# Unit 3's q and k turned by DMA, and a new hand-written order, in a fused gated-recurrence and MLP kernel

## The chip, the cores and the metric

The kernel runs on one core of a Trainium2 chip. The core has five engines that run side by side: TensorE (PE in the profile; it multiplies matrices and writes to PSUM), VectorE (DVE), ScalarE (ACT), GpSimd (POOL) and SyncE (SP, which here issues every transfer). Sixteen DMA engines move the data. PSUM has eight banks of 128 x 512 float32. The metric is the device time of one execution in microseconds; the median of several runs counts.

## The reference

Two stages: a recurrence with a decaying state for each of 4 x 8 heads over 768 steps, and an MLP with a leaky ReLU on its result for 3072 tokens.

```python
B, H, S, D = 4, 8, 768, 48
f = 1.0 / (1.0 + np.exp(-f_logit))
state = np.zeros((B, H, D, D), dtype=np.float32)
for t in range(S):
    state = f[:, :, t, :, None] * state + np.einsum('bhd,bhe->bhde', k[:, :, t], v[:, :, t])
    y[:, :, t] = np.einsum('bhd,bhde->bhe', q[:, :, t], state)
x = np.ascontiguousarray(y.transpose(0, 2, 1, 3)).reshape(B * S, H * D)
h = x @ w_in                        # (3072, 384) @ (384, 2048)
out = np.maximum(0.01 * h, h) @ w_out   # (3072, 2048) @ (2048, 384)
```

## The kernel before

**Units.** The sequence is cut into chunks of 128 steps. The work is 12 units of 256 tokens. Units 0 to 3 are "paired": unit j holds chunks 0 and 1 of batch j. Units 4 to 11 hold one chunk (2 to 5) of two batches. A call names its unit and mostly a half of it (0, 1, or 2 for both).

**One unit.** Loads `Lf Lk Lq Lv` bring f, k, q, v (line 186 for paired units, 190 for the others). ScalarE makes the log gate (`ge`, `gl`: lines 218 and 230). TensorE sums it over the chunk with a triangular matrix (`cs`, lines 239 to 250), ScalarE takes the exponentials (`dec`, lines 258 to 264), and VectorE or GpSimd multiplies them onto k and q (line 270, `k` and `q`; the last number of a call picks the engine: 0 VectorE, 1 GpSimd). The scaled k and q are needed with the head dimension on the partitions, so they are turned:

- by TensorE: `tk`, `tq` (line 304) transpose four blocks each into one PSUM bank, and `ck`, `cq` (lines 317 and 319) copy the bank to SBUF, on ScalarE or VectorE;
- by DMA: `xk`, `xq` (line 324), one transposing transfer from SBUF to SBUF for a whole unit, without TensorE, a bank or a copy.

Then follow the scores (`sc`, line 340 paired, 347 else), the causal mask (`mk`, VectorE, lines 357 and 361), the new state (`pt` on TensorE, `sf` on VectorE, line 466 or 468, `sb` on GpSimd, lines 473 and 476), and the mix of scores, values and earlier state into the unit's output (`mx`, and `ms` for the second chunk of a paired unit, line 378). `xt` (lines 438 and 440) copies that as xT, the input of the MLP.

**MLP of a unit.** Eight calls `up` (line 484, six matmuls each, weight piece g of `w_in`), each followed by a leaky ReLU on ScalarE (`pr`, line 489), then for each half four calls `dn` (line 496, four matmuls each), a copy (`ob`) and a store (`st`, line 511).

**Weights.** `WI` and `WO` load eight pieces each of `w_in` and `w_out` in float32 into the raw buffers of units 4 and 5; `ci` and `co` cast them to bf16. So a `WO` waits for the `ci` of the same place, and the loads of units 4 and 5 wait for the `co`. Raw buffers are six deep: the loads of unit j + 6 wait until unit j is scaled and cast.

**Order.** There is no automatic schedule. One string of words, `order`, is read from left to right, and every word issues its instructions at once on its engine; so the string fixes the order on each engine and of all transfers in SyncE's queue. Each engine runs its own list strictly in order and waits where data or a buffer is not ready. `F_n_512@b` puts n matmuls on zeros into bank b (line 96): work that only keeps TensorE running. The number behind `@` is the PSUM bank. `Z..` clears padding, `M..` makes constants.

Line 329 says where a turned unit lies, whichever way it was turned:

```python
def turn_dma(x):
    def go(j):
        nc.sync.dma_start_transpose(out=turned(j, x), in_=scaled(j, x).rearrange("t a h d -> t (a h d)"))
    return go
...
for word in order.split():
    word, _, on = word.partition("@")
    name, *numbers = word.split("_")
    parts[name](*[int(n) for n in numbers], *[int(n) for n in on.split(".") if n])
```

Of the kernel before, what the change touches and what calls it, by code (L numbers as in the profile page):

```python
# [15 lines left out]
def kernel(  # L16
# [527 lines left out]
    sc_2_0@5.7 mk_2_1_1 dn_0_1_0@0 mk_2_0_0 dn_1_1_0@6 ci_6_1 Lk_3_1 sf_2_0 dn_0_0_0@4 mk_2_0_1 sb_2_0
    dn_1_0_0@5 Lk_3_0 sf_2_1 up_0_6@3 mk_2_1_0 sb_2_1 up_1_6@7 co_2_0 pr_0_6 mx_2_2@1.2 pr_1_6 Lf_4_0 co_3_2
    ms_2 xt_2_0_0 dn_1_0_1 ge_3_1 xt_2_1_0 co_4_1 dn_1_1_1 WO_6 ge_3_0 up_2_2@3 gl_3_0 Lk_4_0 dn_0_1_1 gl_3_1
    co_5_1 pr_2_2 up_2_5@7 WO_7 cs_3_1@1 Lq_3_0 pr_2_5 up_2_6@2 Lq_4_0 up_2_0@3 pr_2_6 dn_0_0_1 pr_2_0 cs_3_0@7
    Lq_4_1 up_2_4@2 dec_3_0 up_2_1@3 k_3_0_0 ge_4_2 co_6_0 dn_0_1_2 gl_4_2 Lf_5_0 dn_1_1_2 pr_2_1 up_2_7@7
# [5 lines left out]
    cs_5_1@1 sb_3_0 mk_3_1_1 dn_2_1_1 Lk_5_1 dec_5_1 sf_3_1 dn_2_1_2 Lk_5_0 sb_3_1 dn_2_1_3 ge_6_2 dn_2_0_3  # L554
    gl_6_2 Lf_8_1 mx_3_2@3.6 ob_2_0_1 st_1_1 ms_3 xt_3_0_0 q_5_2_1 sc_4_2@5.7.4.1 Lq_7_0 xt_3_1_0 cs_6_1@2
    cs_6_0@3 mk_4_1_1 dec_6_1 up_3_3@6 mk_4_0_0 Lf_7_0 up_3_2@1 dec_6_0 mk_4_1_0 up_3_1@2 pr_3_2 mk_4_0_1
    up_3_6@5 Lv_4_0 pr_3_3 k_5_2_1 pr_3_1 up_3_0@3 Lv_4_1 pr_3_6 up_3_7@4 pr_3_0 up_3_5@1 pr_3_7 xq_5 dn_3_1_0@7
    pr_3_5 st_0_1 up_3_4@6 Lf_7_1 dn_3_1_1 pr_3_4 xk_5 dn_3_0_0@2 Lv_5_0 v_4_2_0 dn_3_0_1 dn_3_0_2 Lv_5_1
    dn_3_1_2 ob_2_1_1 dn_3_0_3 st_2_1 ge_7_2 dn_3_1_3 Lf_8_0 pt_4_0@5 gl_7_2 pt_4_1@3 Lv_8_0 sf_4_0 mx_4_2@4.1
    ob_3_1_1 sf_4_1 sb_4_0 sc_5_2@6.0.5.7 xt_4_0_1 cs_7_0@3 xt_4_1_1 mk_5_0_0 cs_7_1@4 sb_4_1 Lk_6_1 dec_7_0  # L560
    up_4_5@1 mk_5_0_1 Lk_6_0 up_4_0@6 dec_7_1 mk_5_1_1 v_5_2_1 mk_5_1_0 up_4_3@0 pr_4_0 up_4_2@3 st_2_0 pr_4_5
    Lq_6_1 pr_4_3 up_4_7@7 Lq_6_0 pr_4_2 up_4_6@4 ge_8_2 st_1_0 up_4_4@5 pr_4_6 up_4_1@6 Lk_7_0 gl_8_2 k_6_2_1
    Lf_10_0 pt_5_1@1 pt_5_0@0 pr_4_1 sf_5_1 mx_5_2@3.4 pr_4_4 sf_5_0 pr_4_7 sb_5_1 dn_4_0_0@6 xt_5_0_0 Lk_7_1
    dn_4_1_0@1 xt_5_1_1 sb_5_0 up_5_3@5 Lv_6_1 up_5_7@0 q_6_2_1 pr_5_3 cs_8_1@7 ob_3_0_1 Lq_7_1 up_5_6@3 pr_5_7
    up_5_0@4 dec_8_1 xk_6 dn_4_1_1 pr_5_6 xq_6 dn_4_1_2 pr_5_0 k_7_2_1 Lf_9_0 up_5_1@5 up_5_5@2 Lv_6_0 pr_5_1
    q_7_2_1 dn_4_1_3 pr_5_5 cs_8_0@0 xk_7 ob_4_1_0 up_5_4@7 dec_8_0 dn_4_0_1 pr_5_4 dn_5_0_0@3 dn_4_0_2 st_3_1
    dn_5_1_0@4 Lk_11_0 Lf_9_1 up_5_2@5 dn_4_0_3 xq_7 pr_5_2 v_6_2_0 sc_6_2@2.1.0.7 ob_4_0_1 dn_5_0_1 mk_6_0_1
    Lv_7_1 dn_5_1_1 mk_6_1_1 dn_5_1_2 mk_6_1_0 Lq_8_1 mk_6_0_0 dn_5_1_3 pt_6_0@5 Lq_8_0 dn_5_0_2 ob_5_1_1 sf_6_0
    ge_9_2 dn_5_0_3 sb_6_0 Lk_8_1 gl_9_2 pt_6_1@6 mx_6_2@1.7 sf_6_1 Lk_11_1 sc_7_2@0.2.4.5 sb_6_1 xt_6_0_1
    cs_9_1@6 xt_6_1_1 mk_7_1_1 cs_9_0@1 dec_9_1 up_6_5@7 mk_7_0_0 Lk_8_0 up_6_2@5 mk_7_0_1 dec_9_0 mk_7_1_0  # L570
    st_3_0 up_6_0@0 pr_6_5 q_8_2_1 Lf_10_1 up_6_3@6 pr_6_2 Lv_7_0 pr_6_0 up_6_4@2 pr_6_3 Lq_10_0 up_6_1@1 pr_6_4
    xq_8 up_6_7@4 pr_6_1 k_8_2_1 dn_6_1_0@7 ob_5_0_0 pr_6_7 dn_6_0_0@5 Lf_11_0 ge_10_2 dn_6_0_1 xk_8 gl_10_2
    v_7_2_1 dn_6_0_2 st_4_0 dn_6_1_1 Lv_8_1 pt_7_0@0 pt_7_1@6 cs_10_0@2 Lk_9_1 sf_7_0 dn_6_1_2 dec_10_0 sf_7_1
    sb_7_0 up_6_6@1 Lv_9_0 cs_10_1@3 pr_6_6 mx_7_2@4.0 sb_7_1 st_5_1 dec_10_1 dn_6_1_3 xt_7_0_1 dn_6_0_3
    xt_7_1_1 Lv_9_1 sc_8_2@6.2.1.3 ob_6_0_1 up_7_1@4 mk_8_0_0 st_4_1 up_7_7@0 mk_8_0_1 pr_7_1 Lq_9_0 mk_8_1_0
    up_7_2@5 pr_7_7 Lv_11_1 mk_8_1_1 up_7_3@6 pr_7_2 Lq_9_1 v_8_2_0 up_7_6@2 pr_7_3 Lf_11_1 up_7_4@4 pr_7_6
    v_9_2_0 pt_8_0@1 pt_8_1@0 pr_7_4 ob_6_1_0 up_7_0@3 Lk_9_0 sf_8_0 up_7_5@5 pr_7_0 sf_8_1 sb_8_0 Lk_10_1
# [51 lines left out]
```

## Time and profile before

| | |
|---|---|
| median of 3 runs | 179.4 us (179.13 to 181.27) |
| the profiled execution | 179.61 us |
| its span, first to last instruction | 177.8 us |
| TensorE matmul busy | 169.4 us, 95% of the span |
| transfers | 34.45 MB in 108186 packets, 152 issues by SyncE |
| transposing transfers | 16 (k and q of units 4 to 11) |

The profile shows one execution, from the first to the last instruction; the 1.8 us between time and span lie around it. "PE" is the matmul, "PEld" the weight load, which runs beside it. A group row gives line, engine, operation, output and input tiles, shape, count, busy time, mean duration in ns, and the idle time in front with what ended it. A window row gives start and end, the length, then the busy time of PE, PEld, DVE, ACT and POOL with instruction counts, the granted clock, the share of the DMA engines and GB/s. In the chain of waits each row is a start, a length, and the work that then set the end. In the timeline a row is a start, a length, the engine, the line and the instruction, and in brackets how long the engine stood before it and for what.

### The profile page before, as it was taken

What the parts mean: (1) busy time and instruction counts of PE and PEld (TensorE: products, weight loads), DVE (VectorE), ACT (ScalarE), POOL (GpSimd) and SP (SyncE); (2) the same over time, 40 slices, a digit from 0 to 9 for tenths busy, and PEclk for the clock granted to TensorE, in tenths of its full rate; (3) what the DMA queues carried; (4) which work ended last, traced back from release to release, by engine and by line L of the source; (5) the groups of instructions that cost most, each with busy time, mean ns of one, the idle gap of its engine ahead of it and who ended that gap; (6) DMA issues with size and microseconds to landing.
All of it is one profiled execution on the core that took longest, in us unless ns stands there. A gap on an engine that the chain in (4) does not pass through costs nothing.

```text
span 177.8 us, 5598 instructions
## 1 busy us (share of the span) xinstructions
PE 169.4 (95%) x2298; PEld 124.3 (70%) x2300; DVE 75.3 (42%) x168; ACT 113.1 (64%) x234; POOL 76.5 (43%) x138
## 2 busy tenths in 40 slices
...
GB/s 131 306 301 313 345 312 305 351 251 307 193 185 120 214 184 182 187 234 217 184 201 235 199 185 131 231 222 213 162 195 244 161 267 4 0 92 0 46 6 131
DMA packets 108186, 34.45 MB, mean 194 GB/s; under 512 B 100992, under 2 KB 107136, under 8 KB 108160
## 3 DMA queue, kind: packets, MB, share of 16 engines
...
q14 instruction: 8, 0.07, 0.1%
HBM read 25.17 MB, written 4.72 MB: 168 GB/s over the span
## 4 chain that ended last, share of the span: by engine, by line
PE 88%; SPq 5%; DMA 2%; issue 2%; ACT 1%; DVE 0%; ACTq 0%
PE ps L496 36%; PE ps L484 36%; PE ps L378 6%; SPq L186 5%; DMA f_raw<-in_f_logit_dram 2%; PE ps L347 2%; PE ps L247 2%; PE ps L304 1%; PE ps L456 1%; PE ps L340 1%; PE ps L451 1%; PE ps L96 1%; PE ps L250 1%; DVE kh L270 0%; ACT e L218 0%
## 5 line engine op out<-in xcount | busy, mean ns | idle before, releaser
L489 ACT ACTIVATE gT<-ps 128x512 bf16<-128x512 f32 x96 | 55.4, 615 | 27.4 <-PE ps L484 25.0
L496 PE MATMUL ps<-w_out,gT 128*128 128x384 bf16 x384 | 69.1, 327 | 0.0
L484 PE MATMUL ps<-xT,w_in 128*128 128x256 bf16 x576 | 68.8, 273 | 0.2 <-ACT xT L438 0.2
L484 PEld LDWEIGHTS <-w_in 128*128 128x128 bf16 x576 | 55.2, 98 | 9.1 <-DVE xT L440 0.2
L496 PEld LDWEIGHTS <-gT 128*128 128x128 bf16 x384 | 36.2, 98 | 21.7 <-ACT gT L489 0.3
L361 DVE TENSOR_TENSOR wm<-ps,ut 128x512 bf16<-128x512 f32 x32 | 20.0, 684 | 8.3 <-PE ps L347 8.3
L473 POOL TENSOR_TENSOR sf<-sf,end 128x192 f32<-128x192 f32 x16 | 8.1, 506 | 32.5 <-DVE sf L468 30.4
L270 POOL TENSOR_TENSOR kh<-k_raw,em 128x768 bf16<-128x768 f32 (+1 forms) x12 | 17.4, 1453 | 7.2 <-DMA k_raw<-in_k_dram 5.2
L468 DVE TENSOR_TENSOR sf<-sf,ps 64x192 f32<-64x192 f32 x32 | 11.2, 350 | 21.3 <-PE ps L456 16.3
L507 DVE COPY osb<-ps 128x384 f32<-128x384 f32 x9 | 4.9, 556 | 35.0 <-PE ps L496 26.6
L270 POOL TENSOR_TENSOR qh<-q_raw,at 128x768 bf16<-128x768 f32 (+1 forms) x10 | 15.0, 1496 | 9.2 <-DMA q_raw<-in_q_dram 8.8
L476 POOL CAST sb<-sf 64x192 bf16<-64x192 f32 x40 | 14.2, 355 | 8.2 <-DVE sf L466 5.7
L505 ACT COPY osb<-ps 128x384 f32<-128x384 f32 x15 | 7.3, 485 | 15.4 <-PE ps L496 8.4
L258 ACT ACTIVATE em<-ps 128x384 bf16<-128x384 f32 x24 | 12.1, 502 | 6.9 <-PE ps L250 3.4
L218 ACT ACTIVATE e<-f_raw 128x384 f32<-128x384 f32 (+1 forms) x16 | 11.0, 696 | 6.3 <-DMA f_raw<-in_f_logit_dram 6.1
L259 ACT ACTIVATE at<-ps 128x384 bf16<-128x384 f32 x24 | 12.1, 505 | 0.8 <-POOL qh L270 0.8
L230 ACT ACTIVATE lf<-e 128x384 bf16<-128x384 f32 (+1 forms) x16 | 10.6, 685 | 0.3
L357 DVE TENSOR_TENSOR wm<-ps,pair_mask 128x512 bf16<-128x512 f32 x16 | 10.4, 686 | 0.6 <-PE ps L340 0.3
L96 PE MATMUL ps<-zeros 128*128 128x512 bf16 x26 | 8.1, 458 | 1.3 <-DVE zeros L92 1.2
L438 ACT CAST xT<-ps 128x384 bf16<-128x384 f32 x13 | 6.2, 520 | 4.0 <-PE ps L378 3.9
L440 DVE CAST xT<-ps 128x384 bf16<-128x384 f32 x11 | 6.0, 572 | 6.0 <-PE ps L378 5.9
L378 PE MATMUL ps<-wm,v 64*32 64x128 bf16 (+1 forms) x256 | 7.5, 218 | 0.9 <-issue 0.9
...
## 6 DMA issues: line engine op xcount, KB each, us to landing
...
```

Of the source, the lines that this page charges most:

```text
L218: nc.scalar.activation(e[:, part], src[:, part], AF.Exp, scale=-1.0)
L230: nc.scalar.activation(dst, src, AF.Ln, bias=1.0)
L258: nc.scalar.activation(ems[j % 2][:, a], t[:, 0:H * D], AF.Exp, scale=1.0)
L259: nc.scalar.activation(ats[j % 2][:, a], t[:, 0:H * D], AF.Exp, scale=-1.0)
L270: eng.tensor_mul(heads(j, to[j % NR], a)[:, :, :, 0:D], raw_heads(j, x, a), decays(j, by, a))
L361: nc.vector.tensor_mul(w, src.rearrange("t (p n) -> t p n", p=P2), ut[:, None, :].to_broadcast([128, P2, 128]))
L378: nc.tensor.matmul(banks[st[j]["py", i]][32 * r:32 * r + 32, 128 * kk:128 * kk + 128], lhsT, rhs, start=(i, r) not in begun, stop=i in las ...
L468: nc.vector.tensor_add(sf[rows], sf[rows], new)
L476: nc.gpsimd.tensor_copy(out=sb[rows, :, y * D:y * D + D], in_=sf[rows])
L484: nc.tensor.matmul(pm[:, i, :], w_in_of(ff, kk), xTs[j % 3][:, kk].rearrange("t a s -> t (a s)"), start=(kk == 0), stop=(kk == NK - 1))
L489: nc.scalar.activation(gTs[j % 3][:, 2 * g:2 * g + 2, :], pm, AF.Prelu, alpha=0.01)
L496: nc.tensor.matmul(po, gTs[j % 3][:, ff, 128 * a:128 * a + 128], w_out_b[ff // 2][:, ff % 2, :], start=(ff == 0), stop=(ff == NF - 1))
```

## The change

Only the string `order` is replaced. The words of both strings name the same loads, gates, scores, mixes, ups, downs and stores, with these differences:

- unit 3 has no `tk_3`, `tq_3`, `ck_3`, `cq_3` (four turns and four copies) but `xq_3` and `xk_3`: 18 transposing transfers instead of 16;
- the fills are 7, 1, 2, 1, 1, 1, 1, 1 in eight places instead of 9, 4, 10, 2, 3 in five: 15 matmuls on zeros instead of 28;
- the order on every engine and in SyncE's queue, the engine of some casts, copies and products, and the banks are chosen anew. At the start the first 18 loads come first in SyncE's queue, as before, and then weight pieces 1, 5, 0, 7 (before: 5, 2, 0, 4, 1); in front of `cs_0_0` GpSimd now has six clears and the masks. Eight ups stand before the turns of unit 2 (`tk_2_1`). The mixes of units 9, 10 and 11 stand further forward.

In the diff every line is a piece of the string.

```diff
--- before.py
+++ after.py
@@ -526,71 +526,71 @@
     order = """
-    Zz F_9_512@7 Zb_1_0_1 Lf_0_1 Zb_2_0_0 Zl_1_0 Zb_2_1_0 Zk_2_1 Zv_1_0 Zq_2_0 Lf_0_0 Zl_2_0 Zb_3_0_1 Zb_0_0_0
-    Zk_0_0 Zq_1_0 Mt Lf_1_1 Zq_0_1 Lq_0_0 Zb_1_1_1 Zk_1_1 Lq_0_1 Zl_0_1 Mu Lf_1_0 ge_0_1 Lk_0_0 Zv_2_1 ge_0_0
-    Zb_3_1_1 Lk_0_1 Ms gl_0_0 Mp_0 Lv_0_1 gl_0_1 Mh Mi Lv_0_0 cs_0_0@0 Zb_0_1_1 ge_1_1 Mo Lf_2_1 Zv_0_1 cs_0_1@1
-    F_4_512@7 dec_0_0 Lv_1_1 Lq_1_1 dec_0_1 q_0_0_0 Lq_1_0 k_0_0_0 ge_1_0 Lk_1_0 gl_1_0 q_0_1_0 k_0_1_1 gl_1_1
-    Lf_2_0 tq_0_0@2 tq_0_1@3 cq_0_0_1 tk_0_0@4 Lv_1_0 cs_1_0@5 v_0_0_1 ck_0_0_1 cq_0_1_0 Lk_1_1 cs_1_1@6 v_0_1_0
-    dec_1_0 tk_0_1@7 WI_5 pt_0_2@0.1 ck_0_1_0 dec_1_1 WI_2 sc_0_0@2.3 sf_0_0 sc_0_1@4.5 F_10_512@7 WI_0 sb_0_0
-    mk_0_0_0 ge_2_1 WI_4 q_1_0_0 k_1_0_1 WI_1 sf_0_1 ge_2_0 Lq_2_0 mk_0_0_1 q_1_1_1 gl_2_0 WI_3 gl_2_1 mk_0_1_0
-    sb_0_1 tq_1_0@7 WI_7 cs_2_0@0 k_1_1_0 cq_1_0_1 tq_1_1@6 cs_2_1@2 dec_2_0 v_1_0_1 mk_0_1_1 tk_1_1@1 tk_1_0@3
-    dec_2_1 v_1_1_0 mx_0_2@4.7 cq_1_1_1 ci_5_0 Lk_2_0 pt_1_2@0.5 ck_1_0_1 xt_0_0_0 ms_0 F_2_512@3 ck_1_1_1
-    sf_1_0 ci_2_1 Lk_2_1 xt_0_1_1 sc_1_0@2.6 sc_1_1@3.4 mk_1_0_1 sb_1_0 up_0_5@1 mk_1_1_0 up_0_2@0 F_3_512@6
-    pr_0_5 mk_1_0_0 ci_0_1 Lv_2_1 pr_0_2 mk_1_1_1 up_0_0@7 sf_1_1 ci_4_1 Lq_2_1 mx_1_2@6.3 pr_0_0 sb_1_1 ci_1_2
-    Lv_2_0 ms_1 xt_1_0_0 up_0_4@1 q_2_0_1 xt_1_1_1 WO_0 up_0_1@2 ci_3_0 pr_0_4 WO_1 up_1_1@0 pr_0_1 up_1_0@4
...
-    dn_0_0_3 Lf_5_1 dec_4_1 dn_2_0_0@2 Lv_3_0 dn_1_0_3 Lv_3_1 ob_0_0_1 q_4_2_1 q_3_1_0 dn_1_1_3 Lq_5_0 Lf_6_1
-    dn_0_1_3 ob_1_1_0 k_4_2_1 tq_3_1@7 xq_4 ob_1_0_0 ob_0_1_1 tk_3_0@3 tq_3_0@1 ge_5_2 ck_3_0_0 up_2_3@4
-    cq_3_0_0 Lf_6_0 tk_3_1@6 gl_5_2 cq_3_1_0 dn_2_1_0@0 v_3_0_1 ck_3_1_0 v_3_1_0 pr_2_3 xk_4 sc_3_0@5.3
-    sc_3_1@1.7 mk_3_0_0 pt_3_2@6.4 mk_3_1_0 dn_2_0_1 mk_3_0_1 cs_5_0@5 st_0_0 dn_2_0_2 dec_5_0 sf_3_0 Lq_5_1
...
-    mk_10_0_1 up_9_0@6 mk_10_0_0 pr_9_6 mk_10_1_1 up_9_2@7 pr_9_0 ob_8_1_0 up_9_7@4 pr_9_2 st_8_1 up_9_3@2
-    ob_8_0_1 pr_9_7 st_8_0 up_9_4@1 pr_9_3 up_9_5@0 pr_9_4 up_9_1@6 pr_9_5 mx_10_2@5.7 pr_9_1 sc_11_2@3.4.2.1
-    xt_10_0_0 dn_9_0_0@0 mk_11_1_0 dn_9_1_0@6 mk_11_0_1 dn_9_1_1 xt_10_1_0 mk_11_0_0 dn_9_1_2 mk_11_1_1
-    up_10_1@5 up_10_4@2 pr_10_1 dn_9_0_1 pr_10_4 up_10_7@4 up_10_2@7 pr_10_7 up_10_6@3 pr_10_2 dn_9_1_3 pr_10_6
-    dn_9_0_2 ob_9_1_0 up_10_3@1 st_9_1 dn_9_0_3 pr_10_3 up_10_5@5 ob_9_0_1 up_10_0@2 st_9_0 pr_10_5 mx_11_2@4.7
...
+    Zz F_7_512@7 Lf_0_0 Lf_0_1 Lf_1_1 Lk_0_1 Lq_0_1 Lf_1_0 Lk_0_0 Lq_0_0 Lf_2_0 Lv_0_0 Lq_1_1 Lv_0_1 Lq_1_0
+    Lk_1_0 Lk_1_1 Lv_1_0 Lv_1_1 Lf_2_1 WI_1 WI_5 WI_0 WI_7 Lq_2_0 Lk_2_1 Lk_2_0 Lq_2_1 WI_2 Lv_2_1 Lv_2_0 WI_3
+    WI_4 Zq_0_0 ge_0_0 Zq_1_0 Zb_3_0_0 Zv_0_0 gl_0_0 ge_0_1 gl_0_1 ge_1_1 gl_1_1 Zq_2_1 Zv_2_1 Zb_1_0_1 Zk_2_0
+    Zl_1_0 Mt Zb_0_1_1 Zb_1_1_1 Zb_0_0_1 Zk_0_0 Zl_2_0 Ms Zl_0_0 Zb_3_1_0 Mu Mp_0 Mh cs_0_0@0 cs_0_1@1 F_1_512@7
+    dec_0_1 cs_1_1@2 k_0_1_0 q_0_1_0 Zb_2_1_1 Zb_2_0_0 dec_0_0 dec_1_1 Mi tk_0_1@3 ck_0_1_0 tq_0_1@4 F_2_512@0
+    cq_0_1_0 sc_0_1@5.6 F_1_512@4 mk_0_1_1 mk_0_1_0 q_0_0_1 tq_0_0@7 cq_0_0_0 v_0_0_0 ge_1_0 gl_1_0 cs_1_0@1
+    F_1_512@6 ge_2_0 gl_2_0 cs_2_0@0 v_0_1_0 dec_1_0 k_1_0_0 k_0_0_1 tk_0_0@3 ck_0_0_1 pt_0_2@4.2 F_1_512@1
+    sf_0_0 sc_0_0@6.5 F_1_512@3 mk_0_0_1 dec_2_0 mk_0_0_0 Zk_1_1 tk_1_0@7 ck_1_0_1 Zv_1_1 q_1_1_1 tq_1_1@1
+    cq_1_1_0 q_1_0_1 tq_1_0@3 cq_1_0_1 k_1_1_1 tk_1_1@0 F_1_512@5 sc_1_0@4.7 mk_1_0_1 mk_1_0_0 v_1_0_1
+    mx_0_2@5.3 ck_1_1_1 sc_1_1@6.0 mk_1_1_1 mk_1_1_0 ge_2_1 sb_0_0 ms_0 sf_0_1 v_1_1_1 pt_1_2@1.7 sf_1_0 gl_2_1
+    cs_2_1@4 xt_0_0_1 xt_0_1_1 ci_0_0 WO_0 ci_1_1 up_0_1@5 WO_1 mx_1_2@0.3 ci_5_1 pr_0_1 up_0_5@6 pr_0_5 sb_1_0
+    ms_1 xt_1_1_1 sf_1_1 up_0_0@2 pr_0_0 Lv_3_0 dec_2_1 ci_7_0 up_0_7@1 pr_0_7 xt_1_0_0 up_1_7@5 up_1_5@7
+    up_1_1@6 up_1_0@3 pr_1_5 pr_1_1 k_2_1_1 tk_2_1@0 ck_2_1_1 WI_6 k_2_0_0 tk_2_0@2 ck_2_0_1 pr_1_0 q_2_1_0
+    tq_2_1@4 pr_1_7 q_2_0_0 tq_2_0@1 ci_2_0 up_0_2@7 up_1_2@6 pr_1_2 Mo cq_2_0_0 sc_2_0@0.2 cq_2_1_0 sc_2_1@1.4
+    mk_2_0_0 WO_5 Lf_3_1 WO_2 sb_1_1 Lv_3_1 Lf_3_0 mk_2_1_0 v_2_1_1 v_2_0_1 pt_2_2@3.5 mk_2_1_1 Lq_3_1 ci_3_1
+    up_0_3@6 pr_0_3 up_1_3@0 WO_3 WO_7 ci_4_1 up_0_4@1 up_1_4@4 pr_0_4 WO_4 sb_0_1 Lk_3_0 sf_2_0 co_0_2 Lf_4_1
+    Lf_4_0 mk_2_0_1 mx_2_2@6.3 Lk_3_1 Lq_3_0 pr_1_4 pr_0_2 sb_2_0 ms_2 xt_2_1_1 sf_2_1 co_1_0 dn_1_1_0@2
+    dn_0_1_0@1 dn_1_0_0@5 dn_0_0_0@4 pr_1_3 xt_2_0_0 up_2_7@6 up_2_3@7 up_2_5@3 up_2_4@0 pr_2_7 up_2_2@6 pr_2_5
+    up_2_1@3 pr_2_3 up_2_0@7 co_5_0 v_3_0_0 sb_2_1 ge_3_1 pr_2_4 v_3_1_0 ci_6_1 up_2_6@0 WO_6 pr_2_1 up_1_6@3
+    gl_3_1 pr_2_2 cs_3_1@6 pr_2_6 up_0_6@0 co_2_1 Lq_4_1 Lq_4_0 co_3_0 dn_0_0_1 dn_0_1_1 dn_1_0_1 dn_1_1_1
+    dec_3_1 k_3_1_0 q_3_1_1 ge_3_0 gl_3_0 cs_3_0@6 dec_3_0 q_3_0_0 xq_3 k_3_0_0 xk_3 co_4_1 dn_1_1_2 Lf_5_0
+    dn_0_1_2 dn_1_0_2 dn_0_0_2 Lf_5_1 pr_0_6 pr_2_0 dn_2_0_0@6 dn_2_0_1 dn_2_0_2 pr_1_6 co_6_1 ge_4_2 gl_4_2
+    cs_4_1@0 dec_4_1 co_7_0 dn_0_1_3 dn_0_0_3 dn_1_0_3 ob_0_1_0 ob_0_0_1 ob_1_0_1 Lk_4_0 Lv_5_0 cs_4_0@7 dec_4_0
+    q_4_2_1 st_0_0 st_1_0 dn_1_1_3 ob_1_1_0 Lv_4_0 Lk_4_1 xq_4 pt_3_2@3.0 sf_3_0 sb_3_0 sc_3_1@1.4 mk_3_1_1
+    st_0_1 Lv_4_1 sc_3_0@5.7 mk_3_0_1 mk_3_0_0 mk_3_1_0 sf_3_1 dn_2_1_0@2 dn_2_1_1 dn_2_1_2 dn_2_1_3 mx_3_2@3.4
...
+    up_8_1@1 up_8_5@5 pr_8_1 up_8_4@4 pr_8_4 pr_8_5 mk_9_0_0 mx_9_2@7.0 xt_9_0_1 xt_9_1_1 up_8_0@1 pr_8_0
+    dn_7_0_3 ob_7_0_0 st_7_0 v_10_2_1 cs_10_0@2 dec_10_0 k_10_2_1 xk_10 q_10_2_1 xq_10 up_8_7@4 pr_8_7 up_8_3@5
+    pr_8_3 up_9_3@7 pr_9_3 up_9_6@0 pr_9_6 up_8_2@1 pr_8_2 pt_8_0@3 sf_8_0 sb_8_0 up_8_6@2 pr_8_6 cs_11_1@4
+    dec_11_1 q_11_2_1 xq_11 pt_9_1@5 sf_9_1 pt_8_1@7 k_11_2_1 xk_11 sf_8_1 sb_8_1 v_11_2_0 pt_9_0@0 sf_9_0
+    sb_9_0 dn_7_1_3 ob_7_1_0 st_7_1 up_9_0@1 pr_9_0 dn_8_1_0@3 up_9_2@2 pr_9_2 up_9_1@5 pr_9_1 up_9_4@4 pr_9_4
+    up_9_7@7 pr_9_7 dn_8_0_0@1 dn_8_0_1 sb_9_1 sc_10_2@0.2.6.5 mk_10_0_0 mk_10_1_1 mk_10_1_0 mk_10_0_1 up_9_5@4
+    pr_9_5 dn_8_1_1 dn_9_0_0@7 dn_9_0_1 sc_11_2@0.5.4.6 mk_11_1_0 mk_11_0_1 mk_11_1_1 mk_11_0_0 dn_8_0_2
+    dn_8_0_3 ob_8_0_0 st_8_0 dn_9_1_0@2 mx_10_2@4.5 xt_10_0_0 xt_10_1_1 mx_11_2@6.0 xt_11_1_0 xt_11_0_1 dn_8_1_2
+    up_10_1@1 pr_10_1 up_10_4@5 pr_10_4 dn_9_0_2 up_11_0@4 pr_11_0 dn_9_1_1 up_11_4@6 pr_11_4 up_11_3@0 pr_11_3
...
     """
```

75 lines of the change are left out of this document (31 added, 44 removed).

## Prediction

> **What bounds the kernel now.** I read the page's busy times and its chain of waits first, then the windows, the chain in order of time, and the timeline of the first 25 us.
>
> ```profile
> PE 169.4 (95%) x2298; PEld 124.3 (70%) x2300; DVE 75.3 (42%) x168; ACT 113.1 (64%) x234; POOL 76.5 (43%) x138
> ...
> PE 88%; SPq 5%; DMA 2%; issue 2%; ACT 1%; DVE 0%; ACTq 0%
> ...
> L489 ACT ACTIVATE gT<-ps 128x512 bf16<-128x512 f32 x96 | 55.4, 615 | 27.4 <-PE ps L484 25.0
> ```
>
> ```profile
> 0.00:24.67 24.67, 19.74 (x373) 12.56 (x375) 16.52 (x50) 17.86 (x42) 17.36 (x51) 1.00 0.98 284
> 24.67:174.64 149.97, 149.70 (x1933) 111.77 (x1926) 58.76 (x119) 94.79 (x192) 59.10 (x87) 1.00 0.82 180
> ```
>
> TensorE has 88% of the chain. In the second window it is busy 149.70 of 149.97 us: from 24.67 us to the last matmul there is nothing to win except by giving it less to do. What can move is the first 25 us, where the busy time includes fills on zeros. Two things count: the time T at which the unbroken stretch begins, and how many `up` calls lie before it.
>
> ```profile
> 0.00:24.67 24.67, 2.31 (x19) 1.69 (x19) 1.00 0.98 284
> ```
>
> ```profile
> 24.73 6.66 PE ps L484 x60
> ...
> 31.39 0.89 PE ps L304 x16
> ...
> 69.48 4.55 PE ps L496 x28
> ...
> 100.37 0.90 PE ps L378 x56
> 101.27 0.55 PE ps L347 x16
> ...
> 157.91 0.90 PE ps L378 x56
> ...
> 174.64 0.48 ACT osb L505
> ```
>
> The row that stands alone is line 484 by itself, up to 24.67 us. An `up` is 6 matmuls, so 3 ups come before the stretch (the 19th matmul opens it). Besides, TensorE has by then done all gate sums of units 0 to 2 and all turns, scores, states and mixes of units 0 and 1. The chain gives its prices: an `up` 6.66/10 = 0.67, a `dn` 4.55/7 = 0.65, a mix 0.90, a score 0.55, sixteen turns 0.89.
>
> **The change, step by step.** The order strings hold the same 96 ups, 96 downs, 12 mixes and 16 scores; the differences are these.
>
> *Turns of unit 3.* Its four TensorE turns (16 matmuls) go: -0.89 us from a full engine, all gained. Their four copies were VectorE's, 42% busy, and gain nothing. In their place SyncE issues two transposes.
>
> ```profile
> qT<-qh SPq DMA_TRANSPOSE x8, 3.7
> kT<-kh SPq DMA_TRANSPOSE x8, 4.0
> ```
>
> ```profile
> 141.07 1.92 SPq L324 DMA_TRANSPOSE qT<-qh  x1
> ```
>
> The last transpose of all took 1.92 us to issue; I take that for each at most, and 4 us to landing. They wait for the scaled q and k of unit 3, and SyncE's loads of units 5 and 4 queue behind them. Adding prices along the new order of TensorE from T = 25.0, the second half of unit 3's gate sum ends at 44.5; after two exponentials (each at most a relu's 0.6) and two VectorE products (each about 0.58, the cast of the same size below) k's transpose is ready at 46.9, issues behind q's at about 48 and lands at 52. The score wants it at 52.7. So the two cost nothing, with 0.7 us in hand; anything later stops TensorE by its excess. Upper end: all of one landing, 4 us.
>
> *Fills.* Before there are 28, now 15. All stand ahead of T, where TensorE waits for others: 0 us, as long as the clock stays up (rivals).
>
> *The first 25 us.* SyncE sends 18 loads of units 0 to 2 first, then four weight pieces, as before but in another order (pieces 1, 5, 0, 7). So I take the landing times of the same places in the queue.
>
> ```profile
> 8.83 0.92 POOL L270 TENSOR_TENSOR kh<-k_raw,em 128x384 bf16<-128x384 f32 x1 [1.39 <-DMA k_raw<-in_k_dram]
> ...
> 13.53 0.92 POOL L270 TENSOR_TENSOR kh<-k_raw,em 128x384 bf16<-128x384 f32 x1 [1.09 <-DMA k_raw<-in_k_dram]
> ...
> 18.01 1.05 POOL L166 CAST w_in<-q_raw 128x768 bf16<-128x768 f32 x1 [0.15 <-DMA q_raw<-in_moe_w_in_dram]
> 19.17 0.81 POOL L476 CAST sb<-sf 64x192 bf16<-64x192 f32 x2
> ```
>
> ```profile
> 17.82 0.55 DVE L166 CAST w_in<-k_raw 128x768 bf16<-128x768 f32 x1
> 18.29 0.58 DVE L440 CAST xT<-ps 128x384 bf16<-128x384 f32 x1
> 18.78 0.72 DVE L466 TENSOR_TENSOR sf<-ps,end 64x192 f32<-64x192 f32 x2
> 19.75 2.48 DVE L357 TENSOR_TENSOR wm<-ps,pair_mask 128x512 bf16<-128x512 f32 x4 [0.25 <-PE ps L340]
> ```
>
> ```profile
> 20.00:25.00 5.00, 4.06 (x100) 2.93 (x99) 3.33 (x7) 2.72 (x5) 3.04 (x6) 1.00 1.11 341
> ```
>
> Three waits on a transfer date the 8th, 15th and 20th load: 8.8, 13.5 and 18.0 us; so the 14th, half of unit 1's k, is there at 13.5 - 0.7 = 12.8. From it VectorE runs without a gap: product k 0.6 (as the 0.58 cast) to 13.4; state 0.72 to 14.1; two masks of 2.48/4 to 15.4; a turn's copy at most 0.58 to 15.9; four masks to 18.4; two state adds 1.44 to 19.9; weight piece 0, 0.55, to 20.4; one state 0.72 to 21.1; piece 7 (landed at 18.0 plus twice 393 KB at 341 GB/s, 20.3) to 21.7; unit 1's xT to 22.3. GpSimd casts unit 1's state for 0.81 after 19.9, so its last mix ends near 21.0. TensorE then does up 0 and up 7 of unit 0 by 22.3 and four ups of unit 1 by 25.0. This T is the choice on which the sum rests. Lower end: two weight pieces fewer in the way of xT and a 14th load at 12.5, 24.2; upper end: each of some ten hand-offs 0.15 us late, 26.5.
>
> At T the new order has done the same set plus 8 ups where the old had 3: 5 x 0.67 = 3.3 us less to do.
>
> *From T on.* Transfers: weight pieces 2, 3 and 4 land later than their ups would like, at about 24.4, 26.8 and 28 (one place in the queue costs 0.6 or 1.15 us at 341 GB/s), but each is cast under 1 us later and wanted at 25.9, 28.2 and 29.5. ScalarE: near 40 us unit 3's gate sums want a bank behind six relus (0.615 each) and two gate halves, and near 49 us unit 4's gate sum stands behind two whole gate passes; I put 0.7 us on these two places, between 0 (ScalarE idles 36% of the span) and 2 (three such waits of one relu each). Later loads: the new order mixes units 9, 10 and 11 earlier, the last at 142.5 us, where the old did it at 157.9. That needs the transposes of unit 11 at about 139, where the old order issued the last at 141.07. See the second rival.
>
> *Sum, against the profiled execution* (span 177.8, time 179.61): matmuls end at 25.0 + 149.97 - 3.3 - 0.89 - 0.27 (the old idle of that stretch) + 0.7 = 171.2. The end is the same copy, store and landing: 177.8 - 174.64 = 3.2, span 174.4. With the 1.8 us around the span, 176.2; the median of the runs is 0.2 below the profiled one: **176.0 us**, 1.9% less.
>
> **Rivals.**
>
> *1. The clock is not up in time.*
>
> ```profile
> 1.19 3.81 PE L96 MATMUL ps<-zeros 128*128 128x512 bf16 x9 [1.19 <-DVE zeros L92]
> ...
> 12.05 2.11 PE L96 MATMUL ps<-zeros 128*128 128x512 bf16 x9 [0.16 <-issue]
> ```
>
> Nine fills take 0.42 us each at the start and 0.23 each at 12 us: TensorE begins at half rate, and 3.8 us of fills brought it up. Now seven fills last 7 x 0.42 = 3.0 us, followed by a hole until GpSimd has made the masks, which it now does after six clears (about 5 us). If the rate stays half for the sparse work up to 18 us, the first links of the chain above are late by some of it, 0.3 to 1 us; if it is still half when the ups begin, another 3.8 us of work is done at half rate, 1.9. Middle: +1.5, so 177.5. For it: fewer fills, one at a time. Against it: the gate sums, turns and scores before 12 us are the same work as before, and the old order too had holes there. [...]
>
> *2. The transfers cannot be brought forward (the slower side).*
>
> ```profile
> SPq L324 <- POOL qh L270: 5.1, 3, 3.6
> SPq L324 <- POOL sf L473: 4.2, 2, 3.0
> SPq L324 <- POOL kh L270: 2.9, 3, 1.3
> ```
>
> SyncE's queue is strict in order. In the old run its transposes stood 12.2 us waiting for GpSimd in these three groups alone, with everything behind them. In the new order the queue after unit 3 sums to about 130 us for the last transpose if nothing waits, and by the gate sum of unit 11 (about 130.3, plus two exponentials of 0.6 and two GpSimd products of at most twice the 0.92 of half a unit) to about 135.2, landing at 139.2. The score of unit 11 is wanted near 139.8. If the queue collects the old 12.2 us of waits instead, that transpose issues at 142 and lands at 146: 6 us of TensorE standing, 182. Above 3.4 us of such standing the gain is gone; above 7 us it is slower by 2%. Against it: the wanted order leaves 2 to 5 us between landing and score at most units, by the same sums.
>
> *3. The lead is lost on the way:* one or two operands or banks that the order packs tightly (unit 3's transposes, 0.7 us in hand; unit 11's, 0.6) come 2 to 3 us late: 178.5 to 179.4, no change. That the turns and fills bring nothing by themselves is part of this.
>
> **How the numbers follow.** About 2%, 3.6 us, is what a measurement of this kernel can tell from no change; it lies at 175.8 and 183.0. My case has 0.66 (own range 174.2 to 177.5; the line at 175.8 cuts it nearly in the middle, 0.34 below and 0.32 above), the clock 0.13, the lost lead 0.12, late transfers 0.09, of which 0.07 beyond 183. Faster 0.34 + 0.02 from a mild form of the clock's case = 0.36; slower 0.07; the rest, 0.57, within. The range leaves out late transfers beyond 179.6 and what would need T below 24.2 and no new idle: 174.0 to 179.6.
>
> **What would show it.** Right: line 484 has some 48 matmuls before 25 us and a full stretch from there; turns of line 304 fall from 64 to 48; transposes from 16 to 18; idle from T to the end under 1.5 us. Wrong: T beyond 26; fills or turns at 0.42 us after 5 us (clock); a wait of line 340 or 347 for a transposed kT or qT of over 1 us; SyncE's transposes waiting longer than 12 us in sum.

## The result, and the profile after

| | before | after |
|---|---|---|
| median (4 runs each) | 179.26 us (179.03 to 181.27) | 185.28 us (184.32 to 186.29) |
| ratio | | 1.031, 95% interval 1.022 to 1.040 |
| the profiled execution, its span | 179.61 us, 177.8 us | 186.29 us, 184.5 us |

The change makes the kernel 3.1% slower. Where some runs of a kernel took over 1.5% longer than its fastest, the ratios and their intervals leave them out, while the medians are of all runs. The page of the changed kernel, beginning with the busy times; the second and third line are the busy tenths of TensorE and of the DMA engines in 40 slices of the span, the fourth is the transfer queue (packets, MB, share of 16 engines), the last the chain of waits:

```profile
PE 168.9 (92%) x2269; PEld 123.3 (67%) x2271; DVE 79.8 (43%) x172; ACT 109.4 (59%) x228; POOL 77.5 (42%) x136
...
PE   6768999999999989999999699989999779999991
...
DMA  5999999999197999999989999999978561011022
...
q1 hardware_dynamic: 110272, 34.61, 80.5%
...
PE 48%; SPq 15%; DMA 13%; POOL 10%; DVE 5%; issue 4%; ACT 3%; POOLq 0%; ACTq 0%
```

TensorE's part of the chain has fallen from 88% to 48%. SyncE's queue, transfers and GpSimd have taken it. The windows of the changed kernel, cut where the turns of unit 2 begin and at the last matmul; then line 484 alone in the first of them:

```profile
0.00:27.67 27.67, 22.27 (x390) 15.39 (x393) 21.51 (x56) 19.47 (x44) 17.69 (x47) 0.94 0.98 275
```

```profile
27.67:180.70 153.03, 146.60 (x1882) 107.94 (x1879) 58.29 (x117) 89.45 (x184) 59.78 (x90) 1.00 0.80 177
```

```profile
0.00:27.67 27.67, 5.76 (x48) 4.32 (x48) 0.94 0.98 275
```

The matmuls end at 180.70 instead of the 171.2 forecast. The 9.5 us divide into three: the stretch begins 2.67 late (27.67 for 25.0); TensorE stands 153.03 - 146.60 = 6.43 us in it, 5.7 more than forecast (it stood 0.27 before); its work there is 146.60 instead of 149.97 - 0.27 - 3.3 - 0.89 = 145.5, 1.1 more, for which no row gives a cause. Where it stands, and where SyncE does, from the waits of the changed kernel (sum, times, longest):

```profile
PE ps L347 <- DMA kT<-kh: 3.0, 2, 1.6
...
PE ps L347 <- DMA qT<-qh: 1.3, 2, 1.0
```

```profile
SPq L324 <- DVE qh L270: 6.1, 1, 6.1
```

SyncE's queue at two places, from the changed kernel's timeline:

```profile
41.97 1.00 SPq L190 DMA_DIRECT2D q_raw<-in_q_dram  x2
49.25 1.34 SPq L324 DMA_TRANSPOSE qT<-qh  x1
50.68 1.28 SPq L324 DMA_TRANSPOSE kT<-kh  x1
...
137.85 1.44 SPq L190 DMA_DIRECT2D v_raw<-in_v_dram  x1
139.39 0.65 SPq L511 DMA_DIRECT2D out_dram<-osb  x1
141.30 1.24 SPq L324 DMA_TRANSPOSE kT<-kh  x1
142.90 4.44 SPq L324 DMA_TRANSPOSE qT<-qh  x2
147.71 1.23 SPq L324 DMA_TRANSPOSE kT<-kh  x1
```

From 42.97 to 49.25 SyncE issues nothing: the first word in its way is unit 3's q transpose, whose product is not ready. Unit 11's k is transposed from 147.71 (its landing follows at 150.76), where the last transpose of the kernel before began at 141.07 and landed at 145.49. Now the windows of the kernel before, up to its last transpose's landing, where the last three numbers are granted clock, DMA share and GB/s:

```profile
5.00:145.49 140.49, 136.56 (x1969) 102.42 (x1970) 68.05 (x147) 96.84 (x206) 72.26 (x120) 1.00 1.01 228
```

```profile
42.97:49.25 6.28, 6.28 (x57) 4.86 (x55) 1.47 (x3) 5.18 (x13) 0.83 (x1) 1.00 0.99 209
49.25:145.49 96.24, 96.05 (x1285) 71.74 (x1284) 41.37 (x89) 63.77 (x134) 47.65 (x68) 1.00 0.99 196
```

and windows of the changed kernel:

```profile
42.90:49.30 6.40, 6.40 (x56) 4.53 (x54) 1.33 (x3) 4.19 (x12) 2.45 (x3) 1.00 0.54 137
```

```profile
42.97:49.25 6.28, 6.28 (x55) 4.41 (x54) 1.28 (x3) 4.07 (x12) 2.45 (x3) 1.00 0.55 138
49.25:150.76 101.51, 95.13 (x1258) 69.58 (x1256) 40.59 (x82) 64.21 (x134) 47.42 (x65) 1.00 0.98 196
```

```profile
5.00:150.76 145.76, 135.72 (x1934) 100.92 (x1936) 70.81 (x146) 95.42 (x204) 72.60 (x116) 0.99 0.98 223
```

In the kernel before, the 16 DMA engines are full on the mean of the 140 us up to the last transpose's landing (share 1.01; a value over 1 says that the measure is rough). TensorE was not the only bound: over this stretch the transfers were a second one. In the changed kernel the share falls to 0.54 while SyncE stands, 6.40 x 0.46 = 2.9 us of all engines lost.

These windows account for the late landing. Behind 49.25 us both kernels move 196 GB/s up to their last transpose's landing, and the changed kernel needs 101.51 us for it instead of 96.24. The 5.27 us more are 1.03 MB at that rate: 0.45 MB were not moved while SyncE stood (138 GB/s instead of 209 for 6.28 us), and 0.52 MB are the two added transposes (34.61 MB instead of 34.09).

### The profile page after: what moved, and what is told of

It reads as the page before. It is cut to its first block, busy times and chain, and to the rows that moved or that the text cites. A ratio compares the mean times of both kernels' runs of the same rounds, so it can differ in the third digit from the quotient of the medians.

```text
span 184.5 us, 5521 instructions
## 1 busy us (share of the span) xinstructions
PE 168.9 (92%) x2269; PEld 123.3 (67%) x2271; DVE 79.8 (43%) x172; ACT 109.4 (59%) x228; POOL 77.5 (42%) x136
## 3 DMA queue, kind: packets, MB, share of 16 engines
q1 hardware_dynamic: 110272, 34.61, 80.5%
## 4 chain that ended last, share of the span: by engine, by line
PE 48%; SPq 15%; DMA 13%; POOL 10%; DVE 5%; issue 4%; ACT 3%; POOLq 0%; ACTq 0%
PE ps L496 23%; PE ps L484 17%; SPq L190 8%; DMA k_raw<-in_k_dram 6%; SPq L186 4%; POOL qh L270 4%; POOL kh L270 3%; PE ps L378 3%; DMA v_raw<-in_v_dram 3%; DMA qT<-qh 2%; DMA kT<-kh 2%; SPq L511 2%; SPq L324 1%; PE ps L347 1%; PE ps L304 1%
## 5 line engine op out<-in xcount | busy, mean ns | idle before, releaser
L489 ACT ACTIVATE gT<-ps 128x512 bf16<-128x512 f32 x96 | 54.0, 609 | 28.6 <-PE ps L484 27.6
L507 DVE COPY osb<-ps 128x384 f32<-128x384 f32 x16 | 8.9, 557 | 43.7 <-PE ps L496 29.4
L270 POOL TENSOR_TENSOR kh<-k_raw,em 128x768 bf16<-128x768 f32 (+1 forms) x11 | 15.9, 1449 | 21.9 <-DMA k_raw<-in_k_dram 10.4
L270 POOL TENSOR_TENSOR qh<-q_raw,at 128x768 bf16<-128x768 f32 (+1 forms) x12 | 16.8, 1409 | 18.5 <-PE ps L451 8.3
L476 POOL CAST sb<-sf 64x192 bf16<-64x192 f32 x40 | 15.2, 381 | 4.8 <-DVE sf L466 2.5
L276 POOL CAST vb<-v_raw 128x768 bf16<-128x768 f32 (+1 forms) x9 | 6.1, 681 | 21.4 <-DMA v_raw<-in_v_dram 11.9
L438 ACT CAST xT<-ps 128x384 bf16<-128x384 f32 x16 | 8.0, 523 | 10.5 <-PE ps L378 10.2
L259 ACT ACTIVATE at<-ps 128x384 bf16<-128x384 f32 x24 | 12.2, 506 | 0.0
L505 ACT COPY osb<-ps 128x384 f32<-128x384 f32 x8 | 3.9, 488 | 13.0 <-PE ps L496 8.5
L347 PE MATMUL ps<-qT,kT 48*128 48x128 bf16 x128 | 5.0, 217 | 4.2 <-DMA kT<-kh 3.0
L347 PEld LDWEIGHTS <-kT 48*128 48x128 bf16 x128 | 3.8, 94 | 6.4 <-DMA kT<-kh 3.5
```

The costliest lines, as they stand in the source:

```text
L259: nc.scalar.activation(ats[j % 2][:, a], t[:, 0:H * D], AF.Exp, scale=-1.0)
L270: eng.tensor_mul(heads(j, to[j % NR], a)[:, :, :, 0:D], raw_heads(j, x, a), decays(j, by, a))
L476: nc.gpsimd.tensor_copy(out=sb[rows, :, y * D:y * D + D], in_=sf[rows])
L489: nc.scalar.activation(gTs[j % 3][:, 2 * g:2 * g + 2, :], pm, AF.Prelu, alpha=0.01)
```

## The experiments

The edits move words of `order`; in the diffs a line is a piece of the string, and a line of "..." leaves words out. Each ratio is to the kernel before, run on the same chip in turn (its median there 179.7, 180.4 or 179.9 us); a point is 1% of its time. A hole is a time in which SyncE issues nothing.

**1. The hole filled.**

```diff
+ Lk_4_0 Lk_4_1 Lv_4_0 Lv_4_1 Lk_5_0 Lk_5_1
  xq_3 k_3_0_0 xk_3
...
- Lk_4_0 ... Lv_4_0 Lk_4_1 ... Lv_4_1 ... Lk_5_0 ... Lk_5_1
```

> The new order with six loads of units 4 and 5 (Lk_4, Lv_4, Lk_5, both halves) moved in SyncE's queue ahead of xq_3; nothing else is moved. Theory A (the queue stands 6.3 us for unit 3's q, is never idle from there to the end of unit 11's transposes, and so delivers everything 6 us late): the standing shrinks under 1 us, the last transposing transfer issues near 142 instead of 147.7 and the time is 179 to 181. Rival C (the new order asks for transfers earlier than the queue can bring them, hole or not): at least 183. Rival B (only the late start of the unbroken stretch, 27.7 instead of 25.0 us, counts): 184 to 186, unchanged.

Measured: 183.32 us, ratio 1.016 (1.008 to 1.023). The hole is gone (0.17 us), the last transpose issues at 145.14 instead of 147.71, and about half of the loss is gone (the two intervals just touch). So part of the standing was paid at the end, less than its 6 us. From the timeline of TensorE, and a window of the same run:

```profile
57.95 0.88 PE L340 MATMUL ps<-qT,kT 48*64 48x128 bf16 x32 [2.85 <-DMA kT<-kh]
58.77 4.16 PE L496 MATMUL ps<-w_out,gT 128*128 128x384 bf16 x16
```

```profile
58.20:61.60 3.40, 3.40 (x37) 0.50 1.15 278
```

Unit 3's transposes, now behind six loads, stop TensorE for 2.85 us, and then it runs at half clock for 3.4: four `dn` take 4.16 us, not 2.6.

**2. Unit 3 turned by TensorE in the new order.**

```diff
- xq_3 ... xk_3
...
  pr_1_6
+ tq_3_1@3 cq_3_1_0 tk_3_1@7 ck_3_1_0
...
  dn_0_1_3
+ tq_3_0@3 cq_3_0_0
...
  dn_0_0_3
+ tk_3_0@7 ck_3_0_0
```

> The new order with unit 3 turned by TensorE again (four turns, four copies on VectorE, in banks 3 and 7) and no xq_3, xk_3. Theory A: the hole and 2.7 us of issues leave the queue, TensorE gets 0.9 us back to do: 178.5 to 181. Rival C: at least 183. Rival B: 185 to 187.

Measured: 184.80 us, ratio 1.027 (1.022 to 1.033). Nearly nothing, but for a reason that none of the theories had: without the transposes the queue runs on to the next words that must wait, 4.9 us for a weight cast on VectorE and some 5 us more at other words. The hole had moved.

**3. The two DMA turns in the old order.**

```diff
  Lf_6_1
+ xk_3 xq_3
...
- tq_3_1@7 tk_3_0@3 tq_3_0@1 ck_3_0_0 cq_3_0_0 tk_3_1@6 cq_3_1_0 ck_3_1_0
```

> The old order with the other half of the change alone: xk_3 and xq_3 instead of four turns and four copies, placed in SyncE's queue just before xq_4, where the queue stood 3.7 us. If a DMA turn costs only where the queue has no room (theory A): both fit into that standing and TensorE is rid of 0.9 us, 178.0 to 179. If two more entries delay a queue that is full from there to unit 11 (the stricter form, A2): 180 to 182.

Measured: 183.15 us, ratio 1.015 (1.008 to 1.023). The two transposes fill the hole of 3.7 us, and yet they cost 1.5 points net, 2.7 us: unit 3's score waits 2.69 us for them, half clock follows from 58.24 to 61.65, and the last transpose issues at 143.43 instead of 141.07.

**4. The slow casts at the start.**

```diff
- v_0_0_0 v_0_1_0 q_1_1_1 q_1_0_1
+ v_0_0_1 v_0_1_1 q_1_1_0 q_1_0_0
```

with `k_0_0_1` ahead of `v_0_0_1`, and the two q products ahead of `k_1_0_0`.

> The new order with the casts of unit 0's v on GpSimd and the two products of unit 1's q on VectorE, instead of the other way round. Theory B (VectorE's casts ran two to three times as long beside GpSimd's products, 1.94 and 1.70 us for a half of v instead of 0.8): on VectorE no cast of v stands beside a product, the first state comes 1.5 to 2 us earlier, the turns of unit 2 begin near 26 instead of 27.7, and the time falls by 1 to 2 us to 183 to 184.3. If the casts were slow for another reason: the turns of unit 2 stay at 27 or later and the time within 0.5 us of 185.3.

Measured: 187.23 us, ratio 1.031 (1.024 to 1.037); the two runs behind the ratio took 185.08 and 185.75 us, as the changed kernel. The profiled one took 188.72. In it the first link came earlier (the first state at 13.35 instead of 15.16 us, the four masks' end at 18.2 instead of 20.95), but the turns of unit 2 did not (28.04). A stop of TensorE of 1.65 us and half clock from 22.83 to 26.24 took the gain. So the casts explain the late first links, and more than the casts kept the stretch from beginning at 25.

**5. Unit 3 by TensorE and no holes.** The kernel of run 2 with

```diff
+ Lk_4_0 Lk_4_1 Lv_4_0 Lv_4_1 Lk_5_0 Lk_5_1
  Lf_5_0
...
+ co_4_1
  q_3_1_1
...
  co_3_0
+ co_7_0
```

(these words are taken from further back).

> The new order with unit 3 turned by TensorE again, and now also with the holes of the transfer queue filled: six loads of units 4 and 5 stand ahead of unit 5's gate load, and the two weight casts that they wait for run earlier. Theory Q (SyncE's queue of transfers is a second bound beside TensorE, about 0.95 us for each entry, and each us in which it stands before 45 us to the end is paid there): of the 10.5 us of standing in the run without these moves some 7 us or more go, the last transpose is issued near 140 to 142 us, time 178.5 to 180.5. Theory C (the new order asks for its transfers too early in any case, standing or not): 182 or more.

Measured: 182.44 us, ratio 1.009 (1.005 to 1.013). Two thirds of run 2's loss were the holes. In the profiled run, which took 185.04 us and so more than the other nine, TensorE's longest stop is at the end: VectorE's state add, which frees the score's bank, was behind the cast of unit 11's v, the queue's last load (landed at 139.94):

```profile
144.40 0.40 PE L347 MATMUL ps<-qT,kT 48*128 48x128 bf16 x8 [2.50 <-DVE sf L468]
```

**6. Four loads ahead instead of six.** As run 1, without `Lk_5_0 Lk_5_1`.

> The changed kernel with only four loads (k and v of unit 4) ahead of unit 3's first transpose, instead of the six of the earlier run. Theory Q: the queue still does not stand over 1 us there, unit 3's transposes are issued about 1.7 us earlier than with six loads ahead, so that TensorE waits about 1 us for them instead of 2.85 and keeps its clock, and the end is set by the queue's sum: 182 to 183.3. Rival (the loss of the earlier run was TensorE's wait of 2.85 us and the half clock behind it): 180.5 to 181.5.

Measured: 184.17 us, ratio 1.019 (1.010 to 1.028). TensorE's wait fell from 2.85 to 1.22 us and its clock stayed up there (1.00 from 55.65 to 62.48), without any gain in time. The stop at unit 3 was not what set the end.

**7. Two more turns in the kernel before.**

```diff
  xk_6
+ xx_6
...
  xq_6
+ xy_6
```

where `xx` and `xy` are the same call as `xk` and `xq` with a spare tile as output.

> The kernel before, in its own order, with nothing changed but two more DMA transposes in SyncE's queue: k and q of unit 6 are turned a second time into tiles that nobody reads, each right behind the first. Theory Q: two entries of 1.37 us and their gaps push all later transfers by 2.7 to 2.9 us; before, the last transpose landed 0.4 us ahead of the score that reads it, so the time rises by 2 to 2.9 us, to 181.3 to 182.5. Rival (TensorE alone is the bound, two more transfers in the queue are hidden): 179.3 to 180.

Measured: four of ten runs took 180.4 to 181.5 us (ratio 1.004, 1.000 to 1.008), the other six 183.4 to 187.2; the median of all is 183.52. In the profiled run (180.41) the last transpose landed at 145.54, as before. Two turns alone can thus be absorbed. What happened in the six longer runs no trace shows, so this run fixes no price.

**8. The stores on another queue.**

```diff
- nc.sync.dma_start(out=out[t:t + C, :], in_=out_tile(j, a))
+ nc.scalar.dma_start(out=out[t:t + C, :], in_=out_tile(j, a))
```

> The changed kernel with its 24 stores issued by ScalarE instead of SyncE; same order of words. The same bytes move, but SyncE's queue holds 24 entries fewer (about 20 us of its 98). Theory Q, with the issue queue as the bound: the 6.3 us of standing at unit 3's q stay, but the queue makes them up before 100 us, no TensorE wait for transposes is left behind 100 us, time 176.5 to 180. Rival D (the 16 DMA engines are what is full, the issue times only show their back-pressure): 183 or more.

Measured: 188.00 us, ratio 1.040 (1.032 to 1.048). The queue with 24 entries fewer came to its last transpose no sooner than that of the changed kernel (147.71):

```profile
147.48 1.23 SPq L324 DMA_TRANSPOSE kT<-kh  x1
```

So SyncE's issue is not the limit: each entry just took longer, and up to the last landing the engines moved 224 GB/s at a share of 1.00, as with all entries in one queue (223 at 0.98). The time itself tells nothing of the queue, since TensorE now waited mostly for ScalarE, which issues the stores here (4.1 us; for transposes 0.9).

**9 to 11. The end of the queue.** A theory that came from run 5: the new order loads k and q of units 10 and 11 last, so that their products and four transposes follow one another after the last load, 139 to 151 us. The order before loads them earlier and puts v loads and stores between the transposes, as its timeline shows:

```profile
134.41 0.42 SPq L190 DMA_DIRECT2D v_raw<-in_v_dram  x1
134.93 1.56 SPq L324 DMA_TRANSPOSE kT<-kh  x1
136.58 0.53 SPq L511 DMA_DIRECT2D out_dram<-osb  x1
137.17 0.44 SPq L190 DMA_DIRECT2D v_raw<-in_v_dram  x1
137.71 1.65 SPq L324 DMA_TRANSPOSE kT<-kh  x1
```

The same edit in three kernels (all words taken from their old places):

```diff
+ Lk_10_1
  Lk_11_0
...
  dec_10_0
+ cs_11_1@4 dec_11_1
  k_10_2_1
+ Lv_10_1 Lv_10_0 Lv_11_1
  xk_10 q_10_2_1
+ Lv_11_0
  xq_10
+ st_7_0
- up_8_7@4 pr_8_7 up_8_3@5 pr_8_3
+ up_8_3@5 up_8_7@4 pr_8_3 pr_8_7
...
  k_11_2_1
+ v_10_2_1
...
  mk_10_0_1
+ v_11_2_0
```

Run 9, in the kernel of run 5:

> The kernel of the run without holes (new order, unit 3 by TensorE, six loads and two weight casts earlier), and now also with another order at the end of the transfer queue: the k and q loads of units 10 and 11 go ahead of their v loads, the v loads stand between the four last transposes as in the kernel before, and what follows from it is moved (two v casts behind the products and masks, one cumulative sum, with its decay, earlier). Theory E (the new order ends its stream with k and q loads whose product and turn are then exposed, 8 us from the last k load's landing to the score): the last transpose is issued at 138 to 141 us instead of 143.5, TensorE's stop of 2.5 us before unit 10's score and the half clock behind it go, time 178.5 to 180. Theory S (the 16 DMA engines are full and only the sum of bytes counts, in whatever order): 180.5 to 182.5, with the stop at a mix that waits for v.

Measured: 181.23 us, ratio 1.004 (1.000 to 1.007).

Run 10, in the kernel of run 6:

> The same new end of the transfer queue in the kernel with the two DMA transposes of unit 3 and four loads ahead of them. If the end order is the larger cause (E): 179.5 to 181.5; its distance to the run with unit 3 on TensorE is the price of the two DMA turns themselves, 1 to 2.5 us by the queue's entries (0.5 MB more at some 200 GB/s and their product's delay), 0 or below if they are hidden. Theory S: 182.5 to 184.5, as without the new end.

Measured: 182.21 us, ratio 1.012 (1.005 to 1.019).

Run 11, in the changed kernel itself:

> The changed kernel with the new end of the transfer queue alone; the queue still stands 6 us for unit 3's q. E with the hole's price added: 182 to 183.5 (the hole costs what it cost before, the end gains 2 to 3 us). If the hole is harmless once the end is in order: 179.5 to 181.5. Theory S: 184.5 to 186.

Measured: 185.25 us, ratio 1.027 (1.021 to 1.033).

Theory E missed its range in all three runs; the times of runs 9 and 11 lie in the range of theory S, that of run 10 between the two. What E foresaw in the queue did come. The timeline of SyncE in run 9:

```profile
136.56 0.76 SPq L190 DMA_DIRECT2D v_raw<-in_v_dram  x1
137.44 2.18 SPq L324 DMA_TRANSPOSE qT<-qh  x1
139.71 0.52 SPq L511 DMA_DIRECT2D out_dram<-osb  x1
140.34 1.30 SPq L324 DMA_TRANSPOSE qT<-qh  x1
141.73 1.27 SPq L324 DMA_TRANSPOSE kT<-kh  x1
```

The last transpose goes at 141.73 instead of 143.46 (run 10: 144.24 instead of 144.94; run 11: 144.23 instead of 147.71). The ratios fall by 0.5, 0.7 and 0.4 points, each time with intervals that overlap, so a gain from the order of the end is likely but not shown by any of the three alone. Run 11 also shows that an earlier last transpose is not enough: 3.5 us earlier brought it next to nothing.

The three ratios also price the parts. Filling most of the hole brings 1.5 points with the new end (runs 11 and 10, intervals apart). How it does so no trace shows: both issue the last transpose at 144.2, and their profiled runs took the same time (184.35 and 184.36 us). Turning unit 3 on TensorE again brings 0.8 (10 and 9; 1.5 us, with intervals that overlap, and the two also differ in two loads and two casts).

**12. The last two stops.** The kernel of run 9 with

```diff
  xq_8
+ Lv_8_1 st_4_0 st_5_1
...
- up_8_7@4
  up_9_6@0
+ up_8_7@4
```

> The best order so far (unit 3 by TensorE, holes filled, new end) with its two remaining stops of TensorE taken up: one v load and two stores go behind unit 8's q transpose (TensorE waited 1.19 us for it), and one up-projection group goes two groups later, so that its bank is free (0.91 us). If TensorE alone is the bound then: 2 us less, 178.5 to 179.5. If the full DMA engines set the end: 180 to 181, with the waits moved to other transposes.

Measured: 184.53 us, ratio 1.018 (1.010 to 1.025), a miss. Both stops went, but the two delayed stores kept their output tiles: ScalarE waited 3.6 us to write one, its relus stood behind, and TensorE with them:

```profile
122.12 0.82 PE L496 MATMUL ps<-w_out,gT 128*128 128x384 bf16 x2 [3.41 <-ACT gT L489]
```

**13 and 14. Fewer bytes.** The 12 loads `Lv_6_0` to `Lv_11_1` taken out, in the changed kernel:

> The changed kernel without the 12 loads of v of units 6 to 11 (2.4 MB of its 34.6, about 12 us of the engines at 200 GB/s; its mixes read v of earlier units, all compute stays). Theory D (the 16 DMA engines are full from 5 to 140 us and the changed kernel's stops behind 60 us are late loads and turns): the last transpose is issued 5 to 10 us earlier, the stops at 100 to 125 and 145 to 155 us go, 179.5 to 182. Rival (waits along the chain of products, decays and masks, which no byte shortens): 184 to 185.5.

Measured: 180.36 us, ratio 1.002 (0.999 to 1.005).

In the kernel before:

> The kernel before without the same 12 loads. Theory D with both bounds in balance before: TensorE has no stop behind 25 us that these bytes could remove, 178.5 to 180.4, the same. If the DMA engines were the only bound before: 3 us or more less.

Measured: 180.74 us, ratio 1.004 (1.000 to 1.007).

With 12 us less to do for the engines the changed kernel's loss of 3% is gone, and the kernel before gains nothing. So late transfers made the changed kernel slower. Run 8 took 24 entries out of the queue without taking bytes out, and the last transpose came no sooner, so it is the bytes and not the number of entries that count. A second way is not separated from this: between 50 and 150 us GpSimd waits 11.9 us for loads of v in the changed kernel and 3.9 us in run 13, and its products for the transposes stand behind these waits. The hole is harmless once the engines have room: SyncE stands 4.66 us for unit 3's q in run 13 too. Of run 13, SyncE's end and the window up to the last transpose's landing:

```profile
140.09 1.24 SPq L324 DMA_TRANSPOSE kT<-kh  x1
```

```profile
5.00:143.15 138.15, 132.97 (x1926) 99.47 (x1928) 70.55 (x145) 95.72 (x204) 72.35 (x116) 0.99 0.93 219
```

## Why the prediction was wrong

**Right.** 48 matmuls of line 484 stand before the stretch, and the turns of line 304 are 48. The seven fills brought TensorE to full rate at 5.2 us in this trace, but that was luck, as is shown under T. The forecast's own signs of being wrong came: T beyond 26, half clock behind 5 us (15.42 to 18.83), and waits of line 347 for a kT of up to 1.6 us.

**Failed: "So the two cost nothing, with 0.7 us in hand".** Only the way from product to score was priced there, and on that way it held, since both ends slipped alike: k's transpose was issued at 50.68 instead of 48, the score came at 55.66 instead of 52.7, and it waited for neither transpose. What was not priced is what stands behind a waiting transpose in SyncE's queue, and the engine time of the two transposes themselves. The queue stood 6.28 us while the engines fell to 54%, and the last transpose landed 5.27 us later than before. Runs 1, 10 and 11 show the price of the hole: some 1.5 points.

**Failed: the sum of the queue, "about 130 us ... if nothing waits".** From k's transpose at 48 us it leaves (130 - 48) / 91 = 0.90 us for each entry up to the last transpose. From 50.68 to 147.71 the changed kernel took 1.07 us for each of the same 91, and the kernel before had taken 1.03 (85 entries from 53.54 to 141.07); with 1.03 the sum gives 142. The engines were full, so each entry takes its share of them. The page of the kernel before said as much, in a line that the prediction does not use:

```profile
q1 hardware_dynamic: 108160, 34.09, 82.8%
```

82.8% of 177.8 us are 147 us of all 16 engines, some 142 of them (140.49 x 1.01) up to the last transpose's landing at 145.49: there was next to nothing to bring forward. The second rival had this outcome, late transposes and 182 us, and got a chance of 0.09. Its cause was another: it let old waits of 12.2 us come back, but the timeline of the kernel before shows SyncE standing for 3.71 us (from 49.83 to 53.54) and under 0.3 us at any other place from there to the last transpose. Its argument against itself ("the wanted order leaves 2 to 5 us") rested on the same sum as the forecast.

**Failed: T.** 27.67 for 25.0. Timeline of VectorE in the changed kernel, then of GpSimd:

```profile
11.14 1.10 DVE L276 CAST vb<-v_raw 128x384 bf16<-128x384 f32 x1
12.16 1.00 DVE L282 CAST v<-v_raw 128x64 bf16<-128x64 f32 x2
13.08 0.35 DVE L276 CAST vb<-v_raw 128x384 bf16<-128x384 f32 x1
13.34 1.35 DVE L282 CAST v<-v_raw 128x64 bf16<-128x64 f32 x2
```

```profile
11.11 1.90 POOL L270 TENSOR_TENSOR qh<-q_raw,at 128x384 bf16<-128x384 f32 x2
13.24 0.96 POOL L270 TENSOR_TENSOR kh<-k_raw,em 128x384 bf16<-128x384 f32 x1 [0.24 <-DMA k_raw<-in_k_dram]
```

The same cast takes 1.10 us beside a product of GpSimd and 0.35 when it starts beside an idle GpSimd. The prediction has no term for these casts, which stand ahead of unit 1's product on VectorE: it lets the product begin when its load is there, at 12.8. It began at 14.62, and the first state came at 15.16 instead of 13.4. In these rows each slow cast starts while a product is under way (those at 11.14 and 12.16 us beside the two from 11.11 to 13.01, that at 13.34 beside the one from 13.24 to 14.20); why it is slow there, no trace shows. Half clock from 15.42 to 18.83 added to it, and run 4 shows that removing one of the two is not enough.

That half clock is the first rival's case, and the fills may have a part in it. The changed kernel and runs 1, 2, 5, 6 and 8 to 13 have the same words up to unit 2's turns, so their traces show one start eleven times. Only in run 12 did TensorE run at full rate from 5.5 us on, and there the stretch begins at 25.84, between the forecast's 25.0 and its upper end of 26.5. In the other ten TensorE ran at half clock for at least 3.4 us between 5.5 and 28 us, and the stretch begins at 26.89 to 29.39. In runs 1, 2, 8, 9 and 10 the seven fills did not bring the clock up before about 10 us. With nine fills (the kernel before and runs 3, 7 and 14) it was up by 7.0 us. From the timelines of TensorE, the first turn of the changed kernel (full rate), the same turn in run 1 (half), and the first turn of unit 2 in run 12:

```profile
7.76 0.40 PE L304 MATMUL ps<-ident,kh 128*128 128x128 bf16 x4 [0.41 <-DVE kh L270]
```

```profile
7.73 0.61 PE L304 MATMUL ps<-ident,kh 128*128 128x128 bf16 x4
```

```profile
25.84 0.61 PE L304 MATMUL ps<-ident,kh 128*128 128x128 bf16 x8
```

How the 2.67 us divide between casts and clock stays open: the first state of run 13 came as early as that of run 12 (13.93 and 13.98), and its stretch began at 27.20, behind a stop of 1.48 us whose cause the profile does not name. No run put the fills back.

**The lead and the turns: nearly right in size, but spent.** In run 13, with the transfers out of the way, the stretch begins and ends so (timeline of TensorE, then the chain in order of time):

```profile
27.20 0.61 PE L304 MATMUL ps<-ident,kh 128*128 128x128 bf16 x8
```

```profile
165.46 9.12 PE ps L496 x56
174.58 0.02 issue
```

It is 174.58 - 27.20 = 147.38 us long, 2.6 less than the 149.97 of before: the forecast 3.3 and 0.89, less a stop of 1.26 us near 66 us and some 0.3 us that no row explains. But it begins 2.5 later than 24.67. So the new order only reaches the time of the old even there; the rest of the loss, 5 us, is what the transfers add (185.28 against 180.36 us).

**Not settled.** The price of two DMA turns by themselves: the runs give 0.4 (run 7), 0.8 (9 and 10) and 1.5 points (run 3), with intervals that overlap. No version was found that beats the kernel before; the nearest is run 9.
